# K cache units loaded as 64 KB rows through a ring of three regions, with one V unit split in two

## The chip, the cores and the metric

The kernel runs on one core of a Trainium2 chip. The metric is the device time of one execution in microseconds (us): three runs of the kernel before gave 345.5, 345.55 and 345.85, median 345.55. One further execution was taken by the hardware profiler; it took 345.38 us, of which the profile's span covers 344.0, so 1.38 us lie around the span.

## The reference: what is computed

One decode step of attention for two batch entries, 32 heads, head size 128 and 4096 cached positions, mixed by a gate with a small dense layer. All inputs are bf16.

```python
g = sigmoid((x * gate_w).sum(-1, keepdims=True))       # x: 2 x 1 x 512
q = (x @ wq)                                           # 32 heads of 128
p = softmax(einsum("bhqd,bhkd->bhqk", q, k) * 128**-0.5)
a = einsum("bhqk,bhkd->bhqd", p, v) reshaped @ wo
b = max(x @ w1, 0) @ w2
return g * a + (1 - g) * b
```

The K cache and the V cache hold 2 x 32 x 4096 x 128 values each, 67.1 MB each. The weights add some 11 MB. Every byte of the caches is read once and used for two operations.

## The kernel before, in words

**Units.** Each cache is cut into eight units of 32768 rows of 128 values, 8.39 MB: batch entry u // 4, and eight heads. `unit_in` (L226) lays a unit over 128 partitions, so that one partition gets 64 KB which are contiguous in memory.

**The landing place.** `kv` (L115) holds four slots of 32 KB per partition. K comes in 16 transfers of half a unit each (L237 to L240), so in rows of 32 KB with 64 KB from one row's start to the next; transfer n goes to slot n % 4. The query weights wq land in slot 3 first, so transfer 3 waits until they are used (`pe_qr1`). From n = 4 on, a transfer waits until both transposes of the half that had its slot are done (`kt_...`). V's units 0 to 6 come whole, as 64 KB rows, alternately into slots 0 and 1 and into slots 2 and 3 (L241 to L243); unit u waits for the matmuls of unit u - 2 (`pe_v_...`). V's unit 7 comes as two halves (L244 to L246). Behind it stand wo in two pieces (L247, L248) into slot 0, after `pe_v_6`, and the five pieces of w2 (L249 to L251).

**The queue.** All these loads are issued by SyncE (SP), in the order written. An issue that waits on a semaphore holds up all issues behind it; transfers already issued go on.

**K's stage** (the loop at L496). For each half h of the head size in each half unit, 32 pieces in all, `k_turn` (L349) lets VectorE (DVE) transpose 128 x 4096 f32 words (pairs of bf16 values) from `kv` into one of the NKT = 3 buffers of `kt`. `k_scores` (L357) then runs 16 matmuls of 128 x 512 on TensorE (PE): four weights, each loaded once and held for four banks (the held ones are L195, the one that loads is L375). The scores of all units gather in banks 0 to 3. A transpose waits for the matmuls of the piece three before it. `qbuf` holds the queries in a padded form for four units of two halves; ScalarE (ACT) writes the second batch entry's queries in `q_second` (L323), behind the units that it replaces.

**Between.** `softmax` (L380) takes maxima, exponentials and transposed probabilities; `spread` (L403) lays one unit's probabilities into `ptm`.

**V's stage** (the loop at L505). `v_unit` (L416) runs 64 matmuls per unit, `v_extract` (L431) and `o_gather` (L448) collect. At the end `project` (L468) and `ffn_f` (L477) apply wo and w2, and the output is sent.

The order of all engines is written out by hand; there is no scheduler.

Of the kernel before, what the change touches and what calls it, by code (L numbers as in the profile page):

```python
# [3 lines left out]
dt = mybir.dt  # L4
ALU = mybir.AluOpType
ACT = mybir.ActivationFunctionType
# [7 lines left out]
NKT = 3  # L14
# [71 lines left out]
def bass_gated_mix__gqa_block_cached__dense_activation_relu__decode_kernel(  # L86
# [14 lines left out]
    sb = nc.alloc_sbuf_tensor  # L101
# [10 lines left out]
    ez1 = sb("ez1", [128, 2], dt.float32)  # L112
    gb = sb("gb", [128, 2], dt.float32)
    gm = sb("gm", [128, 2], dt.float32)
    kv = sb("kv", [128, 4, 16384], dt.bfloat16)  # L115
    kt = sb("kt", [128, NKT, 4096], dt.float32)
    qrow = sb("qrow", [128, 2, 4, 128], dt.bfloat16)
    qbuf = sb("qbuf", [128, 8, 4, 160], dt.bfloat16)
    ptm = sb("ptm", [128, 2, 256, 4, 2], dt.bfloat16)
    mpad = sb("mpad", [128, 32], dt.float32)  # L120
    mrow = sb("mrow", [128, 32], dt.float32)
# [15 lines left out]


    flat = kt[:, :, :].rearrange("p k n -> p (k n)")
    kt16 = flat.bitcast(dt.bfloat16).rearrange("p (k r n two) -> p k r n two", k=NKT, r=128, two=2)  # L140
    w1 = flat[:, 0:2752].bitcast(dt.bfloat16)
    E = flat[:, 0:2048].bitcast(dt.bfloat16)
    ET = flat[:, 2048:4096].bitcast(dt.bfloat16)
    w2 = flat[:, 4096:4096 + 2816].bitcast(dt.bfloat16).rearrange("p (r n) -> p r n", n=512)
    X2 = flat[:, 7168:7168 + 1024].rearrange("p (u d) -> p u d", d=128)
    Y = flat[:, 8192:8192 + 512]
    YW = flat[:, 8704:8704 + 512]

    PSF = nc.alloc_psum_tensor("PS", [128, 4096], dt.float32)
    PSB = PSF[:, :].bitcast(dt.bfloat16)  # L150
# [1 line left out]
    def psf(p0, p1, c0, n):  # L152
        return PSF[p0:p1, c0:c0 + n]

    BANK = 512
    QR_B = 5
    QT_B = 4
    qT_ps = PSB[0:128, QT_B * 1024:(QT_B + 1) * 1024]
# [15 lines left out]
    sem_k = [nc.alloc_semaphore(f"sem_k{s}") for s in range(4)]  # L174
    sem_v = [nc.alloc_semaphore(f"sem_v{s}") for s in range(3)]

    mk = {}
# [13 lines left out]
    pool, dve, act, pe, sp = (adder(e) for e in ("pool", "dve", "act", "pe", "sp"))  # L191

    def held(e, out, lhsT, rhs, start, stop):
# [9 lines left out]
         waits=["c_i16z"], signal="c_i16")  # L203
# [5 lines left out]
         waits=["c_i32z"], signal="c_i32")  # L209
# [6 lines left out]
         waits=["c_s4z"], signal="c_s4")  # L216
# [4 lines left out]
    wo_in = A_wo.rearrange("(p r) n -> p (r n)", r=32)  # L221
# [7 lines left out]
    region = kv[:, :, :].rearrange("p (g s) n -> p g (s n)", g=2)  # L229
    wq_sb = kv[:, 3, :].rearrange("p (t u h e d) -> p t u h e d", t=4, u=4, h=4, e=2)  # L230
    wo_sb = kv[:, 0, :]

    act(lambda e: e.dma_start(x_sb[0:2, :], A_x.rearrange("b s d -> (b s) d")).then_inc(sem["x"], 16))
    act(lambda e: e.dma_start(x_sb[2:3, :], gate_w.rearrange("(o d) -> o d", o=1)).then_inc(sem["gw"], 16))
    sp(lambda e: e.dma_start(kv[:, 3, :], wq_in).then_inc(sem["wq"], 16))
    sp(lambda e: e.dma_start(w1, w1_in).then_inc(sem["w1"], 16))
    for n in range(16):  # L237
        u, hf = divmod(n, 2)
        sp(lambda e, n=n, u=u, hf=hf: e.dma_start(kv[:, n % 4, :], unit_in(k_rows, u)[:, 16384 * hf:16384 * (hf + 1)]).then_inc(sem_k[n % 4], 16),
           waits=([f"kt_{2 * (n - 4) + 1}"] if n >= 4 else ["pe_qr1"] if n == 3 else []))  # L240
    for u in range(7):  # L241
# [7 lines left out]
    sp(lambda e: e.dma_start(w2[0:96, 10, :], B_w2[1280:1376, :]).then_inc(sem["w2a"], 16))  # L249
# [41 lines left out]
    def q_proj():  # L291
# [18 lines left out]
        for half in range(2):  # L310
            for j in range(4):
                pe(lambda e, half=half, j=j: e.transpose(qT_ps[:, (4 * half + j) * 128:(4 * half + j + 1) * 128],
                                                         qrow[:, half, j, :], ident16[:, :]),
                   waits=([f"qrow{half}{e2}" for e2 in range(2)] if j == 0 else []),
                   signal=("pe_q" if half and j == 3 else None))
        cols = qT_ps.rearrange("p (f j s m) -> p f s j m", f=2, j=4, s=4)
        for hq in range(4):
            act(lambda a, hq=hq: a.activation(
                out=qbuf[32 * hq:32 * hq + 32, :, :, 32 + 32 * hq].rearrange("p (f s) j -> p f s j", f=2),
                in_=cols[32 * hq:32 * hq + 32, :, :, :, 0], func=ACT.Copy),  # L320
                waits=["pe_q", "c_qbuf"], signal=f"q_0_{hq}")

    def q_second(u):  # L323
        cols = qT_ps.rearrange("p (f j s m) -> p f s j m", f=2, j=4, s=4)
        for hq in range(4):
            act(lambda a, hq=hq: a.activation(  # L326
                out=qbuf[32 * hq:32 * hq + 32, 2 * u:2 * u + 2, :, 32 + 32 * hq],
                in_=cols[32 * hq:32 * hq + 32, u // 2, 2 * (u % 2):2 * (u % 2) + 2, :, 1], func=ACT.Copy),
                waits=[f"pe_sc_{4 * u + 3}"], signal=f"q_1_{u}_{hq}")

    def ffn_h():
        for ft in range(11):
# [14 lines left out]
                signal=f"dve_h{b}")  # L347

    def k_turn(i):  # L349
        n, h = divmod(i, 2)  # L350
        pairs = kv[:, n % 4, :].bitcast(dt.float32).rearrange("p (r h d) -> p h r d", h=2, d=32)
        dst = kt[:, i % NKT, :].rearrange("p (r n) -> p r n", n=32)
        dve(lambda v: v.transpose(out=dst, in_=pairs[:, h]),  # L353
            waits=([f"pe_sc_{i - NKT}"] if i >= NKT else ["pe_h"] if i == 0 else []),
            dwaits=([(sem_k[n % 4], 16 * (n // 4 + 1))] if h == 0 else []), signal=f"kt_{i}")

    def k_scores(i):  # L357
        n, h = divmod(i, 2)
        u, hf = divmod(n, 2)
        for two in range(2):  # L360
            for e2 in range(2):
                pos = 4 * u + 2 * hf + e2
                w = qbuf[:, 2 * (u % 4) + e2, 2 * h + two, 32 - pos:160 - pos]
                first, last = i == 0 and two == 0 and e2 == 0, i == 31 and two == 1 and e2 == 1
                for bk in range(4):
                    head = two == 0 and e2 == 0 and bk == 0
                    waits = [f"kt_{i}"] if head else []
                    if head and i % 4 == 0:
                        waits += [f"q_{u // 4}_{u % 4}_{hq}" if u >= 4 else f"q_0_{hq}" for hq in range(4)]

                    def fn(e, bk=bk, w=w, e2=e2, two=two, first=first, last=last):
                        args = (psf(0, 128, bk * BANK, 512), w, kt16[:, i % NKT, 32 * bk:32 * bk + 32, 16 * e2:16 * e2 + 16, two])
# [3 lines left out]
                    pe(fn, waits=waits, signal=(f"pe_sc_{i}" if two == 1 and e2 == 1 and bk == 3 else None))  # L376
        if i % 4 == 3 and u < 4:
            q_second(u)

    def softmax():  # L380
        dve(lambda v: v.tensor_reduce(out=mpad[:, 0:1], in_=psf(0, 128, 0, 2048), axis=AX.X, op=ALU.max),  # L381
            waits=["pe_sc_31", "c_mpad"], signal="dve_m")
# [32 lines left out]

    def v_unit(u):  # L416
        rows = region[:, u % 2, :].rearrange("p (m c d) -> p m c d", c=4, d=128)
        for m in range(64):
            t = m % 4
            waits, dwaits = [], []  # L420
            if m == 0:
                waits = [f"pt_{u}_{hq}" for hq in range(4)] + ([f"dve_y{u - 2}"] if u >= 2 else [])
                dwaits = [(sem_v[u % 2], 16 * (u // 2 + 1))]
            if u == 7 and m == 32:
                dwaits = [(sem_v[2], 16)]
            pe(lambda e, m=m, t=t: e.matmul(  # L426
                psf(32 * t, 32 * t + 32, V_B[u % 2] * BANK, 512), lhsT=ptm[:, u % 2, 4 * m:4 * m + 4, :, :],
                rhs=rows[:, m], start=(m < 4), stop=(m >= 60), tile_position=(0, 32 * t)),
               waits=waits, dwaits=dwaits, signal=(f"pe_v_{u}" if m == 63 else None))

    def v_extract(u):  # L431
# [60 lines left out]
    gate()  # L492
    selectors()
    q_proj()
    ffn_h()
    for i in range(32):  # L496
        k_turn(i)
        if i >= 1:
            k_scores(i - 1)
    k_scores(31)  # L500
    softmax()
    denominators()
    spread(0)
# [55 lines left out]
```

## Time and profile before

| what | value |
|---|---|
| median of three runs | 345.55 us |
| the profiled execution | 345.38 us |
| its span | 344.0 us |
| busy share of the span: PE, DVE, ACT, POOL | 55%, 51%, 6%, 6% |
| bytes read from HBM | 145.43 MB |
| DVE transposes of K: count, mean of one | 32, 4.424 us |
| weight loads of the score matmuls: count, mean | 128, 0.098 us |
| last transfer of w2 landed, output sent | about 341.7 us, 342.7 us |

How to read it: engines show busy time, and PE's matmuls are pipelined, so 55% is not a share of its peak. The row of DMA in the page is the mean busy share of 16 DMA engines. A landing is seen in the profile as the start of the instruction that waited for it: a transpose for a K transfer, the first matmul of a unit for a V transfer. Differences of such starts tell how far apart two transfers landed.

### The profile page before, as it was taken

Reading aid. Unit: us, or ns where it says so; the run is one execution under the profiler, and the core shown is the slowest. Engines: PE = TensorE matmul, PEld = TensorE weight load, DVE = VectorE, ACT = ScalarE, POOL = GpSimd, SP = SyncE. Lnnn points to the kernel's source line nnn. Section 1 sums busy time; section 2 is a strip of 40 time slices with the busy share of each in tenths; the row PEclk is TensorE's granted clock in tenths of the full one; section 3 lists DMA queues with packets and bytes.
Section 4 is the critical chain, followed back from the end, with each engine's and each line's share of the span. In section 5 each row is a group of like instructions: output and inputs, shape, how many; then the busy total and the mean of one; then the engine's idle time right before and its main releaser. Section 6 shows DMA issues by size and latency. Waiting matters only on the chain.

```text
span 344.0 us, 2352 instructions
## 1 busy us (share of the span) xinstructions
PE 189.3 (55%) x1226; PEld 40.5 (12%) x842; DVE 176.2 (51%) x94; ACT 19.4 (6%) x50; POOL 21.6 (6%) x33
## 2 busy tenths in 40 slices
PE   0432979877787789877875073314070613215264
PEld 0230000000000000000000021102030201002121
DVE  0718888888988888889985730202010030201021
ACT  1130000000000000000000700000000000000000
POOL 8300000000000000000000130101010010100000
PEclk9965899999999999999999565658567565858567
DMA  8999999999999999999999999999999999999995
GB/s 317 457 425 427 427 427 431 434 434 434 440 431 434 431 431 427 427 427 432 462 442 419 472 391 465 404 450 413 434 457 404 472 398 457 419 400 425 433 409 207
DMA packets 4883, 145.57 MB, mean 423 GB/s; under 512 B 549, under 2 KB 906, under 8 KB 1162
## 3 DMA queue, kind: packets, MB, share of 16 engines
q1 hardware_dynamic: 4866, 145.43, 98.5%
q8 instruction: 8, 0.13, 0.2%
q14 instruction: 1, 0.01, 0.0%
q10 hardware_dynamic: 8, 0.00, 0.0%
HBM read 145.43 MB, written 0.00 MB: 423 GB/s over the span
## 4 chain that ended last, share of the span: by engine, by line
DMA 75%; DVE 12%; PE 9%; ACT 1%; issue 1%; SPq 0%; POOL 0%; DVEq 0%
DMA kv<-in_A_k_cache_dram 38%; DMA kv<-in_A_v_cache_dram 27%; DVE kt L353 10%; DMA kt<-in_B_w_dram 7%; PE PS L426 7%; DMA kv<-in_A_wq_dram 4%; ACT kt L396 1%; PE PS L294 1%; PE PS L195 1%; DVE mpad L381 1%; POOL ptm L410 0%; DVE kt L400 0%; PE PS L375 0%; PE PS L481 0%; DVE out_sb L523 0%
## 5 line engine op out<-in xcount | busy, mean ns | idle before, releaser
L353 DVE STREAM_TRANSPOSE kt<-kv 128x4096 f32<-128x4096 f32 x32 | 140.3, 4424 | 19.1 <-DMA kv<-in_A_k_cache_dram 19.1
L195 PE MATMUL PS<-kt,qbuf 128*128 128x512 bf16 x384 | 112.6, 402 | 0.0
L426 PE MATMUL PS<-kv,ptm 128*32 128x512 bf16 x512 | 46.4, 539 | 85.7 <-DMA kv<-in_A_v_cache_dram 84.6
L375 PE MATMUL PS<-kt,qbuf 128*128 128x512 bf16 x128 | 51.8, 405 | 36.3 <-DVE kt L353 36.2
L432 DVE TENSOR_TENSOR kt<-PS,maskc 128x512 f32<-128x512 f32 x8 | 5.5, 692 | 117.6 <-PE PS L426 117.6
L426 PEld LDWEIGHTS PS<-kv,ptm 128*32 128x32 bf16 x512 | 18.6, 128 | 112.1 <-issue 99.7
L375 PEld LDWEIGHTS PS<-kt,qbuf 128*128 128x128 bf16 x128 | 12.5, 98 | 150.5 <-issue 77.0
L410 POOL COPY ptm<-kt 32x512 bf16<-32x512 bf16 x16 | 11.2, 697 | 273.2 <-DVE rsum L440 184.5
L414 ACT ACTIVATE ptm<-kt 32x512 bf16<-32x512 bf16 x8 | 5.1, 654 | 95.3 <-PE PS L426 94.0
L396 ACT ACTIVATE kt<-PS,negm 128x512 bf16<-128x512 f32 x8 | 5.4, 696 | 80.1 <-DVE negm L392 80.1
L436 DVE TENSOR_REDUCE kt<-kt 128x128 f32<-128x512 f32 x8 | 8.2, 1030 | 0.3
L326 ACT ACTIVATE qbuf<-PS 32x8 bf16<-32x8 bf16 x16 | 3.1, 196 | 85.4 <-PE PS L195 85.1
L443 PE MATMUL PS<-rsum,sell 128*32 128x1 f32 x4 | 0.4, 197 | 10.1 <-DVE rsum L440 10.1
L400 DVE STREAM_TRANSPOSE kt<-kt 128x1024 bf16<-128x1024 bf16 x4 | 5.0, 1245 | 1.7 <-ACT kt L396 1.4
L261 PE MATMUL PS<-ident,x_sb 3*128 3x3 bf16 x4 | 0.3, 166 | 8.1 <-POOL s L214 8.1
L264 DVE COPY xT<-PS 128x12 bf16<-128x12 bf16 x1 | 0.2, 171 | 8.4 <-PE PS L261 8.4
L205 POOL MEMSET qbuf<- 128x5120 bf16 x1 | 4.4, 4358 | 0.0
L381 DVE TENSOR_REDUCE mpad<-PS 128x1 f32<-128x2048 f32 x1 | 2.3, 2292 | 4.0 <-PE PS L195 4.0
L294 PE MATMUL PS<-kv,xTw 128*32 128x512 bf16 x32 | 3.3, 584 | 0.6 <-DMA kv<-in_A_wq_dram 0.6
L217 POOL MEMSET ptm<- 128x4096 bf16 x1 | 3.5, 3501 | 0.0
L450 PE MATMUL PS<-kt,selx 128*32 128x128 f32 x16 | 3.1, 330 | 0.6 <-DVE kt L436 0.6
L412 DVE COPY ptm<-kt 32x512 bf16<-32x512 bf16 x8 | 3.1, 387 | 0.2
(63 smaller groups left out, 44.5 us busy)
## 6 DMA issues: line engine op xcount, KB each, us to landing
kv<-in_A_k_cache_dram SPq DMA_DIRECT2D x16, 4096.0 KB, 30.0
kv<-in_A_v_cache_dram SPq DMA_DIRECT2D x2, 4096.0 KB, 28.5
kv<-in_A_wq_dram SPq DMA_DIRECT2D x1, 4096.0 KB, 12.2
kv<-in_A_wo_dram SPq DMA_DIRECT2D x1, 3072.0 KB, 20.9
kt<-in_B_w_dram SPq DMA_DIRECT2D x1, 1376.0 KB, 15.1
kv<-in_A_wo_dram SPq DMA_DIRECT2D x1, 1024.0 KB, 23.4
kt<-in_B_w_dram SPq DMA_DIRECT2D x1, 640.0 KB, 24.2
kt<-in_B_w_dram SPq DMA_DIRECT2D x1, 384.0 KB, 24.7
```

The source lines that it names most:

```text
L195: return e.add_instruction(mybir.InstMatmult(start_tensor_calc=start, stop_tensor_calc=stop, tile_size=(128, 128), tile_position=(0, 0), l ...
L294: pe(lambda e, n=n, t=t: e.matmul(psf(32 * (n % 4), 32 * (n % 4) + 32, (QR_B + n // 4) * BANK, 512), lhsT=xTw[:, t, :], rhs=wq_sb[:, t, n ...
L353: dve(lambda v: v.transpose(out=dst, in_=pairs[:, h]), waits=([f"pe_sc_{i - NKT}"] if i >= NKT else ["pe_h"] if i == 0 else []), dwaits=([ ...
L375: return e.matmul(args[0], lhsT=args[1], rhs=args[2], start=first, stop=last)
L381: dve(lambda v: v.tensor_reduce(out=mpad[:, 0:1], in_=psf(0, 128, 0, 2048), axis=AX.X, op=ALU.max), waits=["pe_sc_31", "c_mpad"], signal=" ...
L396: act(lambda a, bk=bk, e2=e2: a.activation(out=blocks[:, bk, :, 16 * e2:16 * e2 + 16], in_=psf(0, 128, bk * BANK, 512).rearrange("p (r n) ...
L400: dve(lambda v, bk=bk: v.transpose(out=ET[:, 1024 * bk:1024 * bk + 1024], in_=E[:, 1024 * bk:1024 * bk + 1024]), waits=[f"act_exp{bk}{e2}" ...
L410: pool(lambda e, args=args: e.tensor_copy(**args), waits=waits, signal=f"pt_{u}_{hq}")
L414: act(lambda e, args=args: e.activation(func=ACT.Copy, **args), waits=waits, signal=f"pt_{u}_{hq}")
L426: pe(lambda e, m=m, t=t: e.matmul(psf(32 * t, 32 * t + 32, V_B[u % 2] * BANK, 512), lhsT=ptm[:, u % 2, 4 * m:4 * m + 4, :, :], rhs=rows[:, ...
L432: dve(lambda e: e.tensor_tensor(out=Y.rearrange("p (c d) -> p c d", c=4), in0=psf(0, 128, V_B[u % 2] * BANK, 512).rearrange("p (c d) -> p ...
L436: dve(lambda e: e.tensor_reduce(out=X2[:, u, :], in_=Y.rearrange("p (c d) -> p d c", c=4), axis=AX.X, op=ALU.add), waits=[f"dve_y{u}"], si ...
```

## The change

`kv` gets a fifth slot; the three regions of the ring are slot 4 (32 KB), slots 0 and 1 (64 KB) and slots 2 and 3 (64 KB). K comes in ten transfers ("segments") in a new order of units: the halves of units 0 and 7 go through slot 4, and units 1 to 6 go whole, as 64 KB rows, through the two large regions. From the fourth segment on a transfer waits for the last transpose of the segment three before it. V's unit 2 comes in two halves, the first into slot 4 after K's last transpose, the second into slot 0 after the matmuls of V's unit 0. wo goes to slot 4, so that it waits for `pe_v_2`, not `pe_v_6`.

To make room, the buffers of `kt` are half as long: 64 transposes of 128 x 2048, each followed by 8 matmuls with four weight loads, where there were 32 transposes of 128 x 4096, each followed by 16 matmuls with four weight loads. `qbuf` holds two segments' queries and is filled by `q_put`, two segments ahead. `w2` moves to the start of `kt`, and its first piece now waits for the last `spread`.

```diff
-    kv = sb("kv", [128, 4, 16384], dt.bfloat16)
-    kt = sb("kt", [128, NKT, 4096], dt.float32)
+    kv = sb("kv", [128, 5, 16384], dt.bfloat16)
+    kt = sb("kt", [128, NKT, 2048], dt.float32)
-    qbuf = sb("qbuf", [128, 8, 4, 160], dt.bfloat16)
+    qbuf = sb("qbuf", [128, 2, 2, 4, 160], dt.bfloat16)
...
-    wo_sb = kv[:, 0, :]
+    wo_sb = kv[:, 4, :]
+    segments = [(0, (0,)), (1, (0, 1)), (2, (0, 1)), (0, (1,)), (3, (0, 1)), (4, (0, 1)), (7, (0,)), (5, (0, 1)), (6, (0, 1)), (7, (1,))]
+    pieces = []
+    for g, (u, halves) in enumerate(segments):
+        for hf in halves:
+            for h in range(2):
+                for rr in range(2):
+                    pieces.append((g, u, hf, h, rr))
...
+    def place(g):
+        return (4, 0, 2)[g % 3]
...
-    for n in range(16):
-        u, hf = divmod(n, 2)
-        sp(lambda e, n=n, u=u, hf=hf: e.dma_start(kv[:, n % 4, :], unit_in(k_rows, u)[:, 16384 * hf:16384 * (hf + 1)]).then_inc(sem_k[n % 4], 16),
-           waits=([f"kt_{2 * (n - 4) + 1}"] if n >= 4 else ["pe_qr1"] if n == 3 else []))
+    for g, (u, halves) in enumerate(segments):
+        dst = kv[:, 4, :] if len(halves) == 1 else region[:, place(g) // 2, :]
+        src = unit_in(k_rows, u)[:, 16384 * halves[0]:16384 * (halves[-1] + 1)]
+        sp(lambda e, g=g, dst=dst, src=src: e.dma_start(dst, src).then_inc(sem_k[g % 3], 16),
+           waits=([f"kt_{last_of[g - 3]}"] if g >= 3 else ["pe_qr1"] if g == 2 else []))
     for u in range(7):
+        if u == 2:
+            for hf, dst, w in ((0, kv[:, 4, :], "kt_63"), (1, kv[:, 0, :], "pe_v_0")):
+                sp(lambda e, hf=hf, dst=dst: e.dma_start(dst, unit_in(v_rows, 2)[:, 16384 * hf:16384 * (hf + 1)]).then_inc(sem_v[2 - 2 * hf], 16),
+                   waits=[w])
+            continue
         sp(lambda e, u=u: e.dma_start(region[:, u % 2, :], unit_in(v_rows, u)).then_inc(sem_v[u % 2], 16),
-           waits=([f"pe_v_{u - 2}"] if u >= 2 else ["kt_27"] if u == 0 else ["kt_31"]))
+           waits=([f"pe_v_{u - 2}"] if u >= 2 else [f"kt_{last_of[7]}"] if u == 0 else [f"kt_{last_of[8]}"]))
...
-    sp(lambda e: e.dma_start(wo_sb[:, 0:12288], wo_in[:, 0:12288]).then_inc(sem["wo0"], 16), waits=["pe_v_6"])
+    sp(lambda e: e.dma_start(wo_sb[:, 0:12288], wo_in[:, 0:12288]).then_inc(sem["wo0"], 16), waits=["pe_v_2"])
...
-        dve(lambda v: v.transpose(out=dst, in_=pairs[:, h]),
+        dve(lambda v: v.transpose(out=dst, in_=pairs[:, h, 64 * rr:64 * rr + 64]),
...
-                for bk in range(4):
+                for bk in range(2):
```

More of the change, by code (lines that the diff above doesn't have):

```diff
@@ L139, in bass_gated_mix__gqa_block_cached__dense_activation_relu__decode_kernel @@
     flat = kt[:, :, :].rearrange("p k n -> p (k n)")
-    kt16 = flat.bitcast(dt.bfloat16).rearrange("p (k r n two) -> p k r n two", k=NKT, r=128, two=2)
+    kt16 = flat.bitcast(dt.bfloat16).rearrange("p (k r n two) -> p k r n two", k=NKT, r=64, two=2)
     w1 = flat[:, 0:2752].bitcast(dt.bfloat16)
     E = flat[:, 0:2048].bitcast(dt.bfloat16)
[L143 to L147, printed above, removed]
+    ET = flat[:, 4096:6144].bitcast(dt.bfloat16)
+    w2 = flat[:, 0:2816].bitcast(dt.bfloat16).rearrange("p (r n) -> p r n", n=512)
+    X2 = flat[:, 3072:4096].rearrange("p (u d) -> p u d", d=128)
+    qflat = qbuf[:, :, :, :, :].rearrange("p s e j c -> p (s e j c)").bitcast(dt.float32)
+    Y = qflat[:, 0:512]
+    YW = qflat[:, 512:1024]
     PSF = nc.alloc_psum_tensor("PS", [128, 4096], dt.float32)
@@ L173, in bass_gated_mix__gqa_block_cached__dense_activation_relu__decode_kernel @@
     sem = {n: nc.alloc_semaphore("sem_" + n) for n in names}
-    sem_k = [nc.alloc_semaphore(f"sem_k{s}") for s in range(4)]
+    sem_k = [nc.alloc_semaphore(f"sem_k{s}") for s in range(3)]
     sem_v = [nc.alloc_semaphore(f"sem_v{s}") for s in range(3)]
@@ L227, in unit_in @@
         return rows[u * 32768:(u + 1) * 32768, :].rearrange("(p r) d -> p (r d)", p=128)
-    region = kv[:, :, :].rearrange("p (g s) n -> p g (s n)", g=2)
+    region = kv[:, 0:4, :].rearrange("p (g s) n -> p g (s n)", g=2)
     wq_sb = kv[:, 3, :].rearrange("p (t u h e d) -> p t u h e d", t=4, u=4, h=4, e=2)
-    wo_sb = kv[:, 0, :]
+    wo_sb = kv[:, 4, :]
[6 more added lines that the diff above has]
+                    pieces.append((g, u, hf, h, rr))
+    last_of = {p[0]: i for i, p in enumerate(pieces)}
+    first_of = {}
+    for i, p in enumerate(pieces):
+        first_of.setdefault(p[0], i)
+    def place(g):
+        return (4, 0, 2)[g % 3]
     act(lambda e: e.dma_start(x_sb[0:2, :], A_x.rearrange("b s d -> (b s) d")).then_inc(sem["x"], 16))
@@ L246, in bass_gated_mix__gqa_block_cached__dense_activation_relu__decode_kernel @@
            waits=(["pe_v_5"] if hf == 0 else []))
-    sp(lambda e: e.dma_start(wo_sb[:, 0:12288], wo_in[:, 0:12288]).then_inc(sem["wo0"], 16), waits=["pe_v_6"])
+    sp(lambda e: e.dma_start(wo_sb[:, 0:12288], wo_in[:, 0:12288]).then_inc(sem["wo0"], 16), waits=["pe_v_2"])
     sp(lambda e: e.dma_start(wo_sb[:, 12288:16384], wo_in[:, 12288:16384]).then_inc(sem["wo1"], 16))
-    sp(lambda e: e.dma_start(w2[0:96, 10, :], B_w2[1280:1376, :]).then_inc(sem["w2a"], 16))
+    sp(lambda e: e.dma_start(w2[0:96, 10, :], B_w2[1280:1376, :]).then_inc(sem["w2a"], 16),
+       waits=[f"pt_7_{hq}" for hq in range(4)])
     for name, r0, r1 in (("w2b", 0, 5), ("w2c", 5, 8), ("w2d", 8, 9), ("w2e", 9, 10)):
@@ L315, in q_proj, with q_put @@
                    signal=("pe_q" if half and j == 3 else None))
+    def q_put(g):
+        b, u4 = divmod(segments[g][0], 4)
         cols = qT_ps.rearrange("p (f j s m) -> p f s j m", f=2, j=4, s=4)
@@ L318, in q_proj @@
             act(lambda a, hq=hq: a.activation(
[L319 to L329, printed above, removed]
+                out=qbuf[32 * hq:32 * hq + 32, g % 2, :, :, 32 + 32 * hq],
+                in_=cols[32 * hq:32 * hq + 32, u4 // 2, 2 * (u4 % 2):2 * (u4 % 2) + 2, :, b], func=ACT.Copy),
+                waits=(["pe_q", "c_qbuf"] if g < 2 else [f"pe_sc_{last_of[g - 2]}"]), signal=f"q_{g}_{hq}")
     def ffn_h():
@@ L349, in k_turn @@
     def k_turn(i):
-        n, h = divmod(i, 2)
-        pairs = kv[:, n % 4, :].bitcast(dt.float32).rearrange("p (r h d) -> p h r d", h=2, d=32)
+        g, u, hf, h, rr = pieces[i]
+        slot = place(g) + (hf if len(segments[g][1]) == 2 else 0)
+        pairs = kv[:, slot, :].bitcast(dt.float32).rearrange("p (r h d) -> p h r d", h=2, d=32)
         dst = kt[:, i % NKT, :].rearrange("p (r n) -> p r n", n=32)
-        dve(lambda v: v.transpose(out=dst, in_=pairs[:, h]),
+        dve(lambda v: v.transpose(out=dst, in_=pairs[:, h, 64 * rr:64 * rr + 64]),
             waits=([f"pe_sc_{i - NKT}"] if i >= NKT else ["pe_h"] if i == 0 else []),
-            dwaits=([(sem_k[n % 4], 16 * (n // 4 + 1))] if h == 0 else []), signal=f"kt_{i}")
+            dwaits=([(sem_k[g % 3], 16 * (g // 3 + 1))] if i == first_of[g] else []), signal=f"kt_{i}")
     def k_scores(i):
-        n, h = divmod(i, 2)
-        u, hf = divmod(n, 2)
+        g, u, hf, h, rr = pieces[i]
         for two in range(2):
@@ L362, in k_scores @@
                 pos = 4 * u + 2 * hf + e2
-                w = qbuf[:, 2 * (u % 4) + e2, 2 * h + two, 32 - pos:160 - pos]
-                first, last = i == 0 and two == 0 and e2 == 0, i == 31 and two == 1 and e2 == 1
-                for bk in range(4):
+                w = qbuf[:, g % 2, e2, 2 * h + two, 32 - pos:160 - pos]
+                first, last = i < 2 and two == 0 and e2 == 0, i > 61 and two == 1 and e2 == 1
+                for bk in range(2):
                     head = two == 0 and e2 == 0 and bk == 0
                     waits = [f"kt_{i}"] if head else []
-                    if head and i % 4 == 0:
-                        waits += [f"q_{u // 4}_{u % 4}_{hq}" if u >= 4 else f"q_0_{hq}" for hq in range(4)]
+                    if head and i == first_of[g]:
+                        waits += [f"q_{g}_{hq}" for hq in range(4)]
                     def fn(e, bk=bk, w=w, e2=e2, two=two, first=first, last=last):
-                        args = (psf(0, 128, bk * BANK, 512), w, kt16[:, i % NKT, 32 * bk:32 * bk + 32, 16 * e2:16 * e2 + 16, two])
+                        args = (psf(0, 128, (2 * rr + bk) * BANK, 512), w, kt16[:, i % NKT, 32 * bk:32 * bk + 32, 16 * e2:16 * e2 + 16, two])
                         if bk:
@@ L375, in fn @@
                         return e.matmul(args[0], lhsT=args[1], rhs=args[2], start=first, stop=last)
-                    pe(fn, waits=waits, signal=(f"pe_sc_{i}" if two == 1 and e2 == 1 and bk == 3 else None))
-        if i % 4 == 3 and u < 4:
-            q_second(u)
+                    pe(fn, waits=waits, signal=(f"pe_sc_{i}" if two == 1 and e2 == 1 and bk == 1 else None))
+        if i == last_of[g] and g + 2 < len(segments):
+            q_put(g + 2)
     def softmax():
         dve(lambda v: v.tensor_reduce(out=mpad[:, 0:1], in_=psf(0, 128, 0, 2048), axis=AX.X, op=ALU.max),
-            waits=["pe_sc_31", "c_mpad"], signal="dve_m")
+            waits=["pe_sc_63", "c_mpad"], signal="dve_m")
         dve(lambda v: v.transpose(out=mrow[:, :], in_=mpad[:, :]), waits=["dve_m"], signal="dve_mt")
@@ L417, in v_unit @@
         rows = region[:, u % 2, :].rearrange("p (m c d) -> p m c d", c=4, d=128)
+        halves = [kv[:, s, :].rearrange("p (m c d) -> p m c d", c=4, d=128) for s in (4, 0)]
         for m in range(64):
@@ L422, in v_unit @@
                 waits = [f"pt_{u}_{hq}" for hq in range(4)] + ([f"dve_y{u - 2}"] if u >= 2 else [])
[L423 to L426, printed above, removed]
+                dwaits = [(sem_v[2], 16) if u == 2 else (sem_v[u % 2], 16 * (u // 2 + 1))]
+            if u in (2, 7) and m == 32:
+                dwaits = [(sem_v[0], 32) if u == 2 else (sem_v[2], 32)]
+            at = halves[m // 32][:, m % 32] if u == 2 else rows[:, m]
+            pe(lambda e, m=m, t=t, at=at: e.matmul(
                 psf(32 * t, 32 * t + 32, V_B[u % 2] * BANK, 512), lhsT=ptm[:, u % 2, 4 * m:4 * m + 4, :, :],
-                rhs=rows[:, m], start=(m < 4), stop=(m >= 60), tile_position=(0, 32 * t)),
+                rhs=at, start=(m < 4), stop=(m >= 60), tile_position=(0, 32 * t)),
                waits=waits, dwaits=dwaits, signal=(f"pe_v_{u}" if m == 63 else None))
@@ L494, in bass_gated_mix__gqa_block_cached__dense_activation_relu__decode_kernel @@
     q_proj()
+    q_put(0)
+    q_put(1)
     ffn_h()
-    for i in range(32):
+    for i in range(64):
         k_turn(i)
@@ L499, in bass_gated_mix__gqa_block_cached__dense_activation_relu__decode_kernel @@
             k_scores(i - 1)
-    k_scores(31)
+    k_scores(63)
     softmax()
```

## The prediction

> **What bounds the kernel now.** I first read the page's shares and its DMA rows, then the landings, then SP's waits.
>
> ```profile
> PE 189.3 (55%) x1226; PEld 40.5 (12%) x842; DVE 176.2 (51%) x94; ACT 19.4 (6%) x50; POOL 21.6 (6%) x33
> ...
> DMA  8999999999999999999999999999999999999995
> ...
> q1 hardware_dynamic: 4866, 145.43, 98.5%
> q8 instruction: 8, 0.13, 0.2%
> ```
>
> No engine is busy for more than 55% of the span, but the DMA engines are full in every slice but the first and the last, and the loads' queue alone takes 98.5% of 16 engines' time. The bytes cannot change. So the time is the stream of loads, plus some 3 us of end behind it (L481 and the output). The chain of waits agrees: 75% of it is DMA. The question is how dense the stream is, and whether the new order of waits ever leaves it empty.
>
> Density is read from landings. Two K transposes of the timeline, thirteen halves apart, and four first matmuls of V:
>
> ```profile
> 46.96 8.77 DVE L353 STREAM_TRANSPOSE kt<-kv 128x4096 f32<-128x4096 f32 x2 [1.02 <-DMA kv<-in_A_k_cache_dram]
> ...
> 173.23 8.77 DVE L353 STREAM_TRANSPOSE kt<-kv 128x4096 f32<-128x4096 f32 x2 [0.94 <-DMA kv<-in_A_k_cache_dram]
> ...
> 211.99 6.20 PE L426 MATMUL PS<-kv,ptm 128*32 128x512 bf16 x64 [7.80 <-DMA kv<-in_A_v_cache_dram]
> ...
> 308.74 5.61 PE L426 MATMUL PS<-kv,ptm 128*32 128x512 bf16 x64 [14.29 <-DMA kv<-in_A_v_cache_dram]
> 318.47 2.53 PE L426 MATMUL PS<-kv,ptm 128*32 128x512 bf16 x32 [4.11 <-DMA kv<-in_A_v_cache_dram]
> 328.09 3.60 PE L426 MATMUL PS<-kv,ptm 128*32 128x512 bf16 x32 [7.09 <-DMA kv<-in_A_v_cache_dram]
> ```
>
> K's halves in 32 KB rows land (173.23 - 46.96) / 13 = 9.713 us apart, so a unit in two halves takes 19.43. V's whole units in 64 KB rows land (308.74 - 211.99) / 5 = 19.35 us apart (V1 to V6). A unit in one piece is 0.076 us cheaper. The last two lines are V's unit 7 in halves: 9.73 + 9.62 = 19.35, a single sample that shows no such gain. The trace's packet records stand on the other side: a 32 KB row takes 1.217 us on its engine and a 64 KB row 2.422, so two short rows cost 0.012 more; with eight rows per engine that is 0.10 us a unit.
>
> **What the change does to the stream.** Six K units become whole and one V unit becomes two halves: five transfers fewer. At 0.076 us each the stream is 5 x 0.076 = 0.38 us shorter. The ends are 0 (unit 7) and 5 x 0.10 = 0.5. I take 0.076: it is a mean over thirteen and five landings, the others are a single sample and a busy time.
>
> **Does the queue stay full?** I write down the new landings with these intervals, from 27.4 (first transpose at 27.45; the loads up to there are unchanged). A piece of K: the page has transposes of 128 x 32 words at 0.2 us and of 128 x 4096 at 4.424, on a straight line 2048 words take 2.30; two in a row took 8.77, so the next one starts 0.08 before the last ends: 2.22 apart, 8.95 for a half (before 8.77), 17.8 for a unit (7 x 2.22 + 2.30). Both stay below the landings' 9.71 and 19.35. Units land at 46.8 (g1), 66.1 (g2), 75.8, 95.2, 114.5, 124.3, 143.6, 163.0, 172.7 (g9), V0 192.0, V1 211.4, V2a 221.1, V2b 230.8, V3 250.2.
>
> An issue must come before what is already queued has landed:
> - g4 waits for the last transpose of g1: 46.8 + 17.8 = 64.6; the queue is full until g3, 75.8. Cover 11.2 us. g5 (83.9 against 95.2), g7 (113.0 against 124.3), g8 (132.3 against 143.6), V0 (161.4 against 172.7) and V1 (180.8 against 192.0) have the same 11 us; g3, g6, g9 and V2a, which wait for slot 4, more than 20.
> - V2b waits for V0's matmuls. The last transpose ends at 189.7, its 8 matmuls take 1.9 (0.235 us from one to the next in K's stage), then the softmax as before, 11.6 (186.03 to 197.65), and V0's 64 matmuls 6.6: 209.8, against V2a at 221.1. Cover 11.3. Behind V2b in SP's queue stands V3, which waits for V1's matmuls anyway (217.6, against 230.8).
> - V4 waits for V2's second half: 230.8 + 3.5 = 234.4, against 250.2. V5 to V7 are as before.
> - The rest (V7b, wo, w2) is issued at 295, not at 314 to 318; before, V7b covered it until 328. No hole goes, so nothing is gained.
>
> The smallest cover before was V2 (issued at 204.2, V1 landed at 212.0), 7.8 us. So the softmax, 5 to 6 us later than before, costs nothing: V1 lands at 211.4 and V0's matmuls end at 209.8.
>
> **What lies beside the stream, at nothing.** Weight loads of L375: 128 more, 0.098 us each, but a matmul that loads weights takes 0.23 of the chain and a held one 0.24, so they hide in PE's queue; unhidden they would add 0.8 us to the 7.5 that PE needs for a half, under 9.71. ACT's queries: 40 of 0.2 us, written two segments ahead; the first eight at 19.3 us, done long before the first score matmul at 29.7. POOL's memset of `qbuf` halves, 2.2 us less ahead of the first matmuls, which wait for wq (landed at 12.97). `kt` holds three shorter buffers: a piece's 8 matmuls take 1.9 us of the 4.4 that the ring allows. PE's clock was granted at 0.5 from 19.8 on and for the first 4.5 us of scores, 0.42 us a matmul, 3.4 a piece; this comes back after the idle time between the first half and g1 (36.4 to 46.8), costs two or three us there, and g4 has 11. The tail behind the last landing is the same code.
>
> **The rule I weighed.** A transfer with nothing ahead of it, wq, landed 12.24 us after its issue, 2.5 more than the 9.71 of a queued one. If each paid that, five fewer would save 12.6 us (332.6). The queued landings leave no place for it. The Trainium skill's "DMA: Bandwidth & Descriptors" (section "Anatomy of one DMA") fits a transfer as some 2.0 us fixed plus its bytes at 436 GB/s, for DMAs issued by GpSimd; by that the five would be worth 10 us and the time about 335.5 as an estimate. The trace does not agree where the queue is full: 4.194 MB in 9.713 us is 432 GB/s with everything in it.
>
> **The rivals.**
> - No gain, 345.5 (0.09): the 0.076 belongs to K's stage, where DVE and PE read SBUF, and not to the rows. For it: unit 7's halves at 19.35. Against: the packet records show 1.217 in both stages. That 64 KB rows are cut in two on K (0.04) gives the same time; V's rows show 896 packets of 64 KB, so I doubt it.
> - One more instruction fetch, slower, 346.7 (0.07). The eight packets of 16 KB in q8 each go to one DMA engine. After one, in the records, that engine is 1.5 us late (1.10 for the fetch, and its next row 0.46 longer), and since a load lands with its last engine, every landing after the first fetch (23 us) is late by as much: w1 and K's first half, 5.6 MB, took 14.45 us where 432 GB/s gives 12.97. The later ones cost nothing, because each hit an engine not yet hit. PE's 128 more weight loads are half a packet more, so the eighth fetch moves from 338 to about 323, ahead of the end of the stream. It decides if it hits an engine that already had one: 345.2 + 1.5 (or 0.6, if only its bytes at 26 GB/s count). On a ninth engine it is free.
> - K's stage becomes bound by DVE or PE, slower (0.04). DVE would have to use up 11 us of cover over the thirteen halves from g1 to g8, 0.86 each: 2.64 us a piece instead of 2.22. PE at the 0.5 clock throughout needs 13.6 us a half, and some ten halves beyond the cover would cost 39 us (384). Against: before, PE idled 1.4 to 1.5 us in every half and kept its full clock; now it idles about as long once in a unit.
> - A gain beyond 0.7 us (0.05): the early issue of the small loads at the end packs them closer; the slices there hold 340 GB/s, not 430, for some 7 us, 1.4 us at most (343.8). Or every transfer pays a fixed time (0.01, above). Against both: those loads had over 10 us in the queue before, too.
>
> **How the numbers follow.** The forecast has 0.70. The profiled execution would take 344.0 - 0.4 + 1.4 = 345.0; it stood 0.17 below the median of the runs, so the median becomes 345.55 - 0.38 = 345.2. Range 344.8 to 346.0: below, the whole 0.5 and the 0.2 by which runs differ; above, no gain, the runs' upper end (0.3 over the median) and the cheap fetch (345.8). 0.2% is 0.69 us, about what a measurement of this kernel can tell from no change. Forecast, no gain and uncut rows fall within it: 0.83. Faster 0.06, slower 0.11.
>
> **What would show it.** Right: first transposes of whole K units 19.35 us apart; DMA slices full from end to end; SP's issues 11 us ahead of the queue's end; about 4146 packets in q1 (640 rows and 80 completions fewer). Wrong: DMA slices of 8 or less in the middle, first transposes more than 19.4 apart, matmuls of V2 or V3 late, transposes of 2.6 us, or a clock of 0.5 between 60 and 185 us. If all landings shift by 1.5 us after some point, it is the fetch.

## The result, and the profile after

Fifteen runs of each kernel: before 345.7 us (345.38 to 346.23), after 345.13 us (344.77 to 345.32). The ratio is 0.9982, with a 95% interval of 0.9976 to 0.9989: 0.4 to 0.8 us faster. The forecast was 345.2, in a range of 344.8 to 346.0, and a change within 0.2%. The profiled execution took 345.09 us, span 343.8 (before 345.38 and 344.0). Shares and DMA rows of the page after:

```profile
PE 200.2 (58%) x1226; PEld 53.9 (16%) x970; DVE 175.0 (51%) x126; ACT 22.9 (7%) x70; POOL 19.5 (6%) x33
...
DMA  8998989999998999998999999999999999999995
...
q1 hardware_dynamic: 4146, 145.43, 98.4%
q8 instruction: 8, 0.13, 0.2%
```

The reader is to see that nothing else became the bound: the loads' queue moves the same bytes in 720 packets fewer, in 98.4% of 16 engines' time. The K transposes and V's first matmuls in the timeline after (start, busy time, engine, line):

```profile
27.54 8.89 DVE L373 STREAM_TRANSPOSE kt<-kv 128x2048 f32<-128x2048 f32 x4 [4.72 <-DMA kv<-in_A_k_cache_dram]
46.80 17.66 DVE L373 STREAM_TRANSPOSE kt<-kv 128x2048 f32<-128x2048 f32 x8 [10.37 <-DMA kv<-in_A_k_cache_dram]
66.16 26.43 DVE L373 STREAM_TRANSPOSE kt<-kv 128x2048 f32<-128x2048 f32 x12 [1.70 <-DMA kv<-in_A_k_cache_dram]
...
163.01 26.43 DVE L373 STREAM_TRANSPOSE kt<-kv 128x2048 f32<-128x2048 f32 x12 [1.59 <-DMA kv<-in_A_k_cache_dram]
```

```profile
211.68 5.08 PE L447 MATMUL PS<-kv,ptm 128*32 128x512 bf16 x64 [2.58 <-DMA kv<-in_A_v_cache_dram]
221.38 3.57 PE L447 MATMUL PS<-kv,ptm 128*32 128x512 bf16 x32 [4.62 <-DMA kv<-in_A_v_cache_dram]
231.00 3.60 PE L447 MATMUL PS<-kv,ptm 128*32 128x512 bf16 x32 [6.05 <-DMA kv<-in_A_v_cache_dram]
250.45 6.16 PE L447 MATMUL PS<-kv,ptm 128*32 128x512 bf16 x64 [15.85 <-DMA kv<-in_A_v_cache_dram]
...
327.83 3.30 PE L447 MATMUL PS<-kv,ptm 128*32 128x512 bf16 x32 [6.01 <-DMA kv<-in_A_v_cache_dram]
```

The lines of the kernel before against which they are read, beside those shown ahead:

```profile
27.45 8.77 DVE L353 STREAM_TRANSPOSE kt<-kv 128x4096 f32<-128x4096 f32 x2 [4.89 <-DMA kv<-in_A_k_cache_dram]
...
163.52 8.77 DVE L353 STREAM_TRANSPOSE kt<-kv 128x4096 f32<-128x4096 f32 x2 [0.94 <-DMA kv<-in_A_k_cache_dram]
...
250.69 5.63 PE L426 MATMUL PS<-kv,ptm 128*32 128x512 bf16 x64 [14.29 <-DMA kv<-in_A_v_cache_dram]
```

A whole K unit (g2) lands 66.16 - 46.80 = 19.36 us behind g1, where two halves took 19.43. From g1 to g8 there are five whole units and two halves: 116.21 us; the twelve halves between the transposes at 46.96 and 163.52 before took 116.56, so 0.07 us a unit. V's unit 2 in halves gives one unit's gain back: from V1 to V3 38.77 us, before 38.70. From the first K transpose to the last half of V it is 327.83 - 27.54 = 300.29 us, before 328.09 - 27.45 = 300.64: 0.35 us, all of it in the stream of loads.

### The profile page after: what moved, and what is told of

It is laid out like the page before. It is cut to its first block, busy times and chain, and to the rows that moved or that the text cites. A ratio compares the mean times of both kernels' runs of the same rounds, so it can differ in the third digit from the quotient of the medians.

```text
span 343.8 us, 2528 instructions
## 1 busy us (share of the span) xinstructions
PE 200.2 (58%) x1226; PEld 53.9 (16%) x970; DVE 175.0 (51%) x126; ACT 22.9 (7%) x70; POOL 19.5 (6%) x33
## 3 DMA queue, kind: packets, MB, share of 16 engines
q1 hardware_dynamic: 4146, 145.43, 98.4%
## 4 chain that ended last, share of the span: by engine, by line
DMA 76%; DVE 11%; PE 11%; SPq 0%; issue 0%; DVEq 0%
DMA kv<-in_A_k_cache_dram 32%; DMA kv<-in_A_v_cache_dram 28%; DMA kt<-in_B_w_dram 12%; DVE kt L373 10%; PE PS L447 5%; DMA kv<-in_A_wq_dram 4%; PE PS L394 3%; PE PS L196 2%; PE PS L318 1%; SPq L275 0%; DVE kt L457 0%; DVE qbuf L453 0%; DVE out_sb L546 0%; DVE ptm L431 0%; SPq L272 0%
## 5 line engine op out<-in xcount | busy, mean ns | idle before, releaser
L373 DVE STREAM_TRANSPOSE kt<-kv 128x2048 f32<-128x2048 f32 x64 | 141.2, 2274 | 25.4 <-DMA kv<-in_A_k_cache_dram 25.4
L394 PE MATMUL PS<-kt,qbuf 128*128 128x512 bf16 x256 | 107.3, 419 | 33.6 <-DVE kt L373 29.2
L196 PE MATMUL PS<-kt,qbuf 128*128 128x512 bf16 x256 | 106.8, 417 | 0.0
L447 PE MATMUL PS<-kv,ptm 128*32 128x512 bf16 x512 | 48.0, 552 | 78.1 <-DMA kv<-in_A_v_cache_dram 76.9
L453 DVE TENSOR_TENSOR qbuf<-PS,maskc 128x512 f32<-128x512 f32 x8 | 5.5, 691 | 111.5 <-PE PS L447 111.5
L394 PEld LDWEIGHTS PS<-kt,qbuf 128*128 128x128 bf16 x256 | 25.9, 101 | 142.8 <-issue 72.8
L345 ACT ACTIVATE qbuf<-PS 32x8 bf16<-32x8 bf16 x40 | 7.8, 196 | 137.5 <-PE PS L196 136.2
L457 DVE TENSOR_REDUCE kt<-qbuf 128x128 f32<-128x512 f32 x8 | 8.2, 1030 | 0.3
L493 PE MATMUL PS<-kv,oW 128*2 128x512 bf16 x32 | 3.7, 621 | 1.1 <-DMA kv<-in_A_wo_dram 1.1
L333 DVE CAST qrow<-PS 128x256 bf16<-128x256 f32 x2 | 2.4, 1398 | 3.2 <-PE PS L318 3.2
## 6 DMA issues: line engine op xcount, KB each, us to landing
kv<-in_A_v_cache_dram SPq DMA_DIRECT2D x4, 4096.0 KB, 27.5
```

The costliest lines, as they stand in the source:

```text
L196: return e.add_instruction(mybir.InstMatmult(start_tensor_calc=start, stop_tensor_calc=stop, tile_size=(128, 128), tile_position=(0, 0), l ...
L345: act(lambda a, hq=hq: a.activation(out=qbuf[32 * hq:32 * hq + 32, g % 2, :, :, 32 + 32 * hq], in_=cols[32 * hq:32 * hq + 32, u4 // 2, 2 * ...
L373: dve(lambda v: v.transpose(out=dst, in_=pairs[:, h, 64 * rr:64 * rr + 64]), waits=([f"pe_sc_{i - NKT}"] if i >= NKT else ["pe_h"] if i == ...
L447: pe(lambda e, m=m, t=t, at=at: e.matmul(psf(32 * t, 32 * t + 32, V_B[u % 2] * BANK, 512), lhsT=ptm[:, u % 2, 4 * m:4 * m + 4, :, :], rhs= ...
L453: dve(lambda e: e.tensor_tensor(out=Y.rearrange("p (c d) -> p c d", c=4), in0=psf(0, 128, V_B[u % 2] * BANK, 512).rearrange("p (c d) -> p ...
L457: dve(lambda e: e.tensor_reduce(out=X2[:, u, :], in_=Y.rearrange("p (c d) -> p d c", c=4), axis=AX.X, op=ALU.add), waits=[f"dve_y{u}"], si ...
```

## The experiments

Theory "rows": each row of a transfer costs its engine about 0.01 us whatever its length, and the gain is 40 rows an engine saved (five transfers of eight). Rivals: "stage" (short pieces, ring or order make the gain), "end" (the early issue of the last loads), and, left over from the prediction, the instruction fetch and the cover that an issue needs.

**K's whole units in two transfers again**

```diff
-        dst = kv[:, 4, :] if len(halves) == 1 else region[:, place(g) // 2, :]
-        ...
+        for hf in halves:
+            dst = kv[:, place(g) + (hf if len(halves) == 2 else 0), :]
+            src = unit_in(k_rows, u)[:, 16384 * hf:16384 * (hf + 1)]
```

> The changed kernel, but each of K's units 1 to 6 comes in two transfers of 32 KB rows, issued one behind the other, into the same region and with the same waits. Ring, order, pieces and V are those of the changed kernel. Theory 'rows' (the gain is six units in long rows, 0.076 us each by the landings of before): the six are taken back, 0.46 us over the changed kernel, ratio to the kernel before 0.999 to 1.000 (V's unit 2 in halves remains, +0.08). Rival 'stage' (the gain comes from shorter pieces, the other ring or order): no change against the changed kernel, 0.998.

Measured: 345.48 us, ratio to before 0.9993 (0.9985 to 1.0002); 0.35 us over the changed kernel. Two transposes in its timeline:

```profile
47.04 17.66 DVE L374 STREAM_TRANSPOSE kt<-kv 128x2048 f32<-128x2048 f32 x8 [10.61 <-DMA kv<-in_A_k_cache_dram]
...
163.63 26.43 DVE L374 STREAM_TRANSPOSE kt<-kv 128x2048 f32<-128x2048 f32 x12 [1.59 <-DMA kv<-in_A_k_cache_dram]
```

116.59 us from g1 to g8, 0.38 more than in the changed kernel for five units: 0.076 each, as forecast. Ring, pieces and order are unchanged here, and most of the gain is gone. "Stage" falls for that part. (In every cut version the shorter rows also have gaps between them in memory, which whole units have not; a cost of the row and a cost of the jump are not told apart.)

**Short pieces alone, in the kernel before**

```diff
-        dve(lambda v: v.transpose(out=dst, in_=pairs[:, h]),
+        dve(lambda v: v.transpose(out=dst, in_=pairs[:, h, 64 * rr:64 * rr + 64]),
```

(with 64 pieces in the loop and two banks for each, as in the change)

> The kernel before with K's 32 KB transfers and its ring as they were, but with 64 transposes of 128 x 2048 and 8 matmuls behind each, as in the changed kernel. Rows: no change, 1.000, since DVE needs 8.9 us for a half and a half lands every 9.71. Stage: a part of the changed kernel's 0.57 us appears here, ratio 0.998 to 0.999.

Measured: 345.61 us against 345.59, ratio 0.9995 (0.9987 to 1.0004): no change.

**The last loads issued late**

```diff
-    ... then_inc(sem["wo0"], 16), waits=["pe_v_2"])
+    ... then_inc(sem["wo0"], 16), waits=["pe_v_6"])
```

> The changed kernel, but wo, and with it w2 behind it, waits for V's unit 6 as in the kernel before (issue at about 314 instead of 296 us). Rows: no change against the changed kernel, 0.998, as V's last half covers the queue until 328. Rival 'end' (0.2 us or more of the gain come from the early issue at the end): ratio 0.9988 or above.

Measured: 345.08 us, ratio 0.9984 (0.9976 to 0.9993), the changed kernel's time. "End" falls.

**Row or transfer?** Two kernels cut twelve whole units into 16 KB rows, one in two transfers, one in four.

```diff
+    def rows16(ap):
+        quarters = ap.rearrange("p (a b n) -> p b a n", a=2, b=2)
+        return [quarters[:, b] for b in range(2)]
...
+        for d, s in ([(dst, src)] if len(halves) == 1 else zip(rows16(dst), rows16(src))):
```

> The changed kernel, but each of the twelve whole units (K 1 to 6, V 0, 1, 3 to 6) comes in two transfers of 16 KB rows, every other quarter of a partition's 64 KB in each: 32 rows an engine and unit instead of 8, and one transfer more. If the cost belongs to the row (0.0095 to 0.0115 us each): 12 x 24 x that = 2.7 to 3.3 us over the changed kernel, ratio to before 1.006 to 1.008. If it belongs to the transfer (0.076 us each): 12 x 0.076 = 0.9 us, ratio 1.0008. If rows cost nothing: 0.998.

> The same twelve units in four transfers of 16 KB rows: the same rows as the kernel with two transfers, 24 transfers more. Cost by row: 0.2 us over that kernel for the completions (24 x 0.009), ratio 1.006 to 1.009. Cost by transfer: 36 x 0.076 = 2.7 us over the changed kernel, 1.8 over that with two, ratio 1.006. The two kernels together tell row from transfer: equal if by row, 1.8 us apart if by transfer.

Measured: 347.78 us (ratio 1.0063, 1.0048 to 1.0078) and 347.84 us (1.0065, 1.0050 to 1.0080). Whether it is 12 or 36 transfers more makes no difference; 24 rows more per engine and unit do. Two landings of whole V units in the timeline of the kernel with two transfers:

```profile
291.60 5.52 PE L453 MATMUL PS<-kv,ptm 128*32 128x512 bf16 x64 [12.09 <-DMA kv<-in_A_v_cache_dram]
311.17 5.97 PE L453 MATMUL PS<-kv,ptm 128*32 128x512 bf16 x64 [14.05 <-DMA kv<-in_A_v_cache_dram]
```

19.57 us a unit, where the changed kernel has 19.36: 0.21 for 24 rows. Over the run it is (347.78 - 345.13) / 288 rows = 0.0092 us a row. The cost belongs to the row.

**V's unit 2 whole**

```diff
-        if u == 2:
-            ...
-            continue
```

> The changed kernel, but V's unit 2 comes whole into slots 0 and 1, waiting for V's unit 0 (issue at about 209 us, where the queue ends with V1 at 211.5, a cover of 2.4 instead of 11 us). Rows and a cover that is enough: 0.08 us faster than the changed kernel, which can't be told from none, 0.998. If an issue must lead by what wq showed (its landing 2.5 us over a queued one's interval), the cover falls short by 0.1 to 0.5 us, all later landings shift by as much, ratio 0.998 to 1.000.

Measured: 346.95 us (345.85 to 347.87), ratio 1.0035 (1.0025 to 1.0045): slower than the kernel before, outside both expectations. The profiled run is its fastest:

```profile
211.49 5.32 PE L442 MATMUL PS<-kv,ptm 128*32 128x512 bf16 x64 [3.38 <-DMA kv<-in_A_v_cache_dram]
231.77 5.98 PE L442 MATMUL PS<-kv,ptm 128*32 128x512 bf16 x64 [14.96 <-DMA kv<-in_A_v_cache_dram]
251.10 6.54 PE L442 MATMUL PS<-kv,ptm 128*32 128x512 bf16 x64 [13.36 <-DMA kv<-in_A_v_cache_dram]
```

V0's matmuls ended at 208.1, and V2 was issued then (at 208.16), 3.3 us before V1's landing is seen at 211.49; still V2 lands 20.28 us behind V1, 0.93 too late, and that is never made up. The trace's packet records (one for each row, and one of 4 bytes that ends a transfer on each engine) tell why 3.3 was not enough. V1's last rows ended between 208.85 and 210.89 on the 16 engines, and each engine's semaphore update came 0.45 to 0.5 us later. So a landing is seen some 0.6 us after the slowest engine and 2.6 after the fastest one ran dry. V2's first row started at 209.13, 1.0 us behind the issue; at 209.5 only 10 engines had a row to move. The eleven engines that ran dry first stood empty for 0.28 us on average, and their first rows then took 2.94 us instead of 2.42: 0.8 us together. That the unprofiled runs lose more, because V0's matmuls end later when PE's clock is lower (they took 4.92 us here, 5.89 and 6.57 in the two kernels' profiles), is argued, not shown: the granted clocks of the twelve runs (0.794 to 0.827, each a mean over the whole run) do not order with their times.

**V's unit 2 in halves, the second issued later**

```diff
-            for hf, dst, w in ((0, kv[:, 4, :], "kt_63"), (1, kv[:, 0, :], "pe_v_0")):
+            for hf, dst, w in ((0, kv[:, 4, :], "kt_63"), (1, kv[:, 0, :], "pe_v_1")):
```

> The changed kernel, but the second half of V's unit 2 waits for V's unit 1 instead of unit 0: issue at 216.8 instead of 209 us, 4.3 to 4.5 before its predecessor's landing is seen at 221.4. With V's unit 2 whole the issue came 3.4 before, and the next landings were late. By the packet records the last rows of a transfer end some 1.5 us before its landing is seen, and the engines that had no fetch 1.5 before that: the first engine runs dry 3 us before. If that is the point from which it costs: 4.3 is enough, the changed kernel's time, 0.998. If more lead is needed, or an engine that idles at all shows in the end: late landings from V's unit 2 on, ratio 0.999 to 1.003.

Measured: 345.0 us, ten of twelve runs from 344.87 to 345.35, two at 345.79 and 346.47; ratio 0.9991 (0.9981 to 1.0001). In its profile the halves land at 221.22, 230.84 and V3 at 250.28, spaced as in the changed kernel. V2's second half is issued at 216.9, so its first row can start at 217.9; by the packet records the fastest engine has rows of the first half until 218.87. So 4.4 us is enough in most runs; the two late ones may be those in which it was not, which the runs don't show.

**Whole K units without a third region**

```diff
-    for n in range(16):
-        ...
+    for u in range(8):
+        sp(lambda e, u=u: e.dma_start(region[:, u % 2, :], unit_in(k_rows, u)).then_inc(sem_k[u % 2], 16),
+           waits=([f"kt_{4 * u - 5}"] if u >= 2 else ["pe_qr1"] if u == 1 else []))
```

> The kernel before with all eight K units whole, in 64 KB rows, but in the two regions of 64 KB that there were, without a third: each is issued when the unit two before it is transposed, 17.5 us after its landing, where the next lands 19.4 after: a cover of 1.9 us at K's units 2 to 7, V0, V1 and V2. If an issue needs 2.5 us of lead (wq's landing against a queued interval): 0.6 us lost nine times, 5 us over before less 0.6 for eight long units, ratio 1.013. If a cover of 1.9 is enough: 0.6 us faster, ratio 0.998, and the third region of the changed kernel buys nothing.

Measured: 356.36 us (355.73 to 359.75), ratio 1.0331 (1.0269 to 1.0394): more than twice the expected loss. Its K transposes in the timeline, and three stretches of 1 us (the last three columns are PE's granted clock, the DMA share and GB/s; a row is counted whole in the stretch in which it starts, so a share can be over 1):

```profile
56.35 17.42 DVE L352 STREAM_TRANSPOSE kt<-kv 128x4096 f32<-128x4096 f32 x4 [1.99 <-DMA kv<-in_A_k_cache_dram]
79.29 17.42 DVE L352 STREAM_TRANSPOSE kt<-kv 128x4096 f32<-128x4096 f32 x4 [5.51 <-DMA kv<-in_A_k_cache_dram]
98.94 17.42 DVE L352 STREAM_TRANSPOSE kt<-kv 128x4096 f32<-128x4096 f32 x4 [2.23 <-DMA kv<-in_A_k_cache_dram]
120.14 17.42 DVE L352 STREAM_TRANSPOSE kt<-kv 128x4096 f32<-128x4096 f32 x4 [3.77 <-DMA kv<-in_A_k_cache_dram]
```

```profile
53.00:54.00 1.00, 1.00 (x6) 0.10 (x1) 1.00 (x1) 0.00 (x0) 0.00 (x0) 1.00 0.15 66
54.00:55.00 1.00, 1.00 (x6) 0.10 (x1) 0.36 (x1) 0.00 (x0) 0.00 (x0) 1.00 0.01 0
55.00:56.00 1.00, 1.00 (x6) 0.13 (x2) 0.00 (x0) 0.00 (x0) 0.00 (x0) 1.00 2.68 918
```

Unit 2 is issued at 54.4, when unit 1 is transposed, and lands 22.94 us behind it instead of 19.35. In the packet records 13 of 16 engines have no row from 54.4 to 55.4, when the new rows begin; most of these first rows take 2.6 to 3.3 us instead of 2.42, and one engine takes up its first row only at 57.8. Units 2 to 7 lose 0.3 to 3.6 us each. The largest loss falls on no instruction fetch; two others do (108.5 us for the landing at 120.14, 173.7 for that at 180.52). Why one engine came so late after 54.4 stays open. What is shown: with two regions long rows cost 10.6 us; the third is what makes them pay.

**More instructions on PE**

```diff
+    def idle_pe(n):
+        for c in range(n):
+            def fn(e, c=c):
+                args = (psf(0, 128, 6 * BANK, 2), ident16[:, :], ident16[:, 0:2])
+                ...
         v_unit(u)
+        if 1 <= u <= 5:
+            idle_pe(256)
```

> The changed kernel with 256 tiny matmuls (128 x 2 on a held weight, into an unused bank) behind each of V's units 1 to 5, where PE waits for the next landing: 1285 instructions more, so five more fetches of 16 KB. If each fetch goes to an engine that had none: no change, 0.998. If a fetch hits engines at random, some engine is hit once more, +1.5 us, ratio 1.0025. If PE is late with a unit, its waits show it.

> Control for the kernel with 256 tiny matmuls behind V's units 1 to 5 (6.5 us of PE each, 346.65): the same places hold 20 matmuls of 128 x 512 each, so about as much PE time (20 x 0.24 to 0.43 us) with 105 instructions more instead of 1285, less than half a fetch. If the 1.5 us there came from instruction fetches: the changed kernel's time, 0.998. If they came from PE being busy beside the loads or late with a unit: 1.0027 as there.

> The changed kernel with 420 tiny matmuls behind V's units 1 to 5 and 6 behind each K piece: 2546 instructions more, ten fetches more instead of five. If a fetch on an engine that already had one costs 1.5 us of that engine, and the latest engine sets every landing: ten more put at least one engine at three, 1.5 us over the kernel with five, ratio 1.007. If extra fetches stay spread evenly so that none has three: 1.0027 again. If fetches cost nothing: 0.998.

Measured: 346.65 us (1.0027, 1.0015 to 1.0039) with 13 fetches; the control with wide matmuls 345.07 us (0.9982, 0.9973 to 0.9992); 347.75 us (1.0058, 1.0043 to 1.0073) with 18. (The control has nine, the ninth at 340.6 us, when the large transfers are through.) The row of the fetch queue and V's landings of the first of them:

```profile
q8 instruction: 13, 0.21, 0.3%
```

```profile
250.47 6.46 PE L456 MATMUL PS<-kv,ptm 128*32 128x512 bf16 x64 [9.35 <-DMA kv<-in_A_v_cache_dram]
...
270.87 6.50 PE L456 MATMUL PS<-kv,ptm 128*32 128x512 bf16 x64 [6.04 <-DMA kv<-in_A_v_cache_dram]
...
290.31 5.33 PE L456 MATMUL PS<-kv,ptm 128*32 128x512 bf16 x64 [5.11 <-DMA kv<-in_A_v_cache_dram]
...
310.05 5.69 PE L456 MATMUL PS<-kv,ptm 128*32 128x512 bf16 x64 [7.93 <-DMA kv<-in_A_v_cache_dram]
```

Up to 250.47 it stands with the changed kernel; then two intervals are too long: 20.40 and 19.74, 1.4 us together, where PE waits 5 to 9 us for each landing. The control has 4.5 to 5.6 us of PE work in the same places, where the first has 6.5, and loses nothing. So the instructions cost, not the matmuls, and they cost through the loads. The packet records show how, by the records that end a transfer on each engine. When V's unit 3 ends in the first kernel, the last engine finishes 2.14 us behind the first; when unit 4 ends, 9 fetches in, one engine is 3.19 behind, and when unit 6 ends four are 3.2 to 3.7. With 18 fetches eight are 2.9 to 4.1 behind at that point. In the changed kernel no engine is ever more than 2.0 behind, through all eight fetches. So the first seven or eight each made another engine late by about 1.5 us, and the later ones also hit engines that were late already.

The first fetch does the same in every kernel. In the one with short pieces alone it came later (26.6 us; in the kernel before and the changed one 24.3 and 25.4), and there it can be seen by itself:

```profile
26.11 8.89 DVE L353 STREAM_TRANSPOSE kt<-kv 128x2048 f32<-128x2048 f32 x4 [2.92 <-DMA kv<-in_A_k_cache_dram]
37.15 8.89 DVE L353 STREAM_TRANSPOSE kt<-kv 128x2048 f32<-128x2048 f32 x4 [2.16 <-DMA kv<-in_A_k_cache_dram]
46.87 8.89 DVE L353 STREAM_TRANSPOSE kt<-kv 128x2048 f32<-128x2048 f32 x4 [0.82 <-DMA kv<-in_A_k_cache_dram]
```

The first half lands at 26.11, not 27.5; the next 11.04 us later, 1.33 more than 9.71; then the step is regular. In the two kernels with 13 and nine fetches it came at 27.6 and 27.7, and the first half landed at 26.14 and 25.95. No version tried beats the changed kernel beyond its interval.

## Why the prediction was right

- **The stream, 0.38 us.** Confirmed in mechanism and size: 0.07 us a unit in the changed kernel, 0.076 when it is undone, 0.35 over the whole stream, and a row of 0.0092 us (40 rows: 0.37). The packet count came out at the forecast 4146. The chosen 0.076 was nearer than either end. Unit 7's halves at 19.35, which spoke for no gain, were misread: the first matmul of a unit starts 0.13 us after its transfer's last semaphore update, one in the middle of a unit 0.05. From update to update (308.61, 318.33, 328.05) the halves took 19.44, as in K's stage. Unit 2 after shows the same 9.70 and 9.62 in the matmuls, and 19.42 in the updates.
- **The queue stays full.** Confirmed, but the step was mis-sized: it counted cover up to the moment when the landing is seen. The engines run dry 0.6 to 2.6 us before, and a new row starts 1.0 us behind its issue, so the first 3.6 us of cover are needed. (The prediction, and the expectation for the second half issued later, place packets about 1 us too early against the instructions; so "1.5" and "3 us" there, and a fetch at 23 or 338, are 0.6, 2.6, 24.3 and 339.4.) With 11 us this changed nothing; with 3.3 it cost 0.9 us in the profile and 1.8 in the median. The Trainium skill, "DMA: Bandwidth & Descriptors" (section "Anatomy of one DMA"), says of DMAs issued by GpSimd that most of a transfer's fixed time is the wait until its last byte is confirmed. For these loads, issued by SP, the trace does not agree: 1.0 us lies ahead of the first row, 0.45 to 0.5 us between an engine's last record and its semaphore update.
- **The pieces.** 2.274 us a piece and 17.66 a unit, forecast 2.30 and 17.8. The softmax moved as forecast (V0's first matmul at 203.21, forecast 203.2). PE's clock was 0.5 again after the idle time ahead of g1, but g1's transposes took 17.66 us like all others: the two or three us allowed for it were not needed, as the ring of pieces covered them. The rival "K's stage becomes bound" counted on the full clock from there on; in fact it fell to 0.5 three more times, for 3.4 us each (from 98.6, 146.4 and 166.8 us; in the last, matmuls took 0.43 us instead of 0.23). The cover was large enough for that too.
- **The early issue at the end.** Worth nothing, as said.
- **The fetch rival.** The mechanism is real and its price right (1.5 us for five more). It did not occur: the changed kernel still has eight fetches. The eighth came at 331.9 us, 7.5 earlier than before and not 15 as forecast, and nothing moved by it: from the last half of V to the issue of the output it is 14.6 us, before and after. But the reason given, that each fetch meets a new engine, holds for seven or eight of them, not for thirteen. What decides which engine a fetch takes was not settled.
- **The signs.** Two signs of failure appeared without a failure. Slices of 8 in the DMA row stand in K's stage (the fourth, sixth, thirteenth and nineteenth) with the stream as dense as forecast; a 64 KB row is counted in the slice in which it starts, so slices with long rows waver. And PE's clock was at 0.5 at times between 60 and 185 us, the other sign, as said above.

The runs moved by 0.57 us (0.4 to 0.8), the profiled stream by 0.35. The spans that were recorded for the runs tell where the rest lies. Their median is 343.8 us in the fifteen runs after and 344.1 in the 35 runs of the kernel before that belong to the first experiments: 0.3 us, the stream. What lies around the span is 1.27 to 1.35 us after, but 1.33 to 1.96 before, over 1.6 in 12 of the 35 runs. That is also where the runs of before scatter; their spans reach only from 343.9 to 344.4. With K's units cut again in the new kernel the span is back at 344.2 and the rest stays short (1.27 to 1.38). So the rows account for the change within the span, and ring, order and pieces for none of it. Another 0.1 to 0.3 us, which the prediction did not have, lies outside the span; its cause stays open. That the median came out within 0.1 us of the forecast is in part luck: it started from 345.55, the median of three runs, where fifteen gave 345.7, and that part made up the difference.

## What to carry to other kernels

When the queue of loads is never empty, only what each engine moves counts: the rows, and anything else on the same engines. Count rows, price them from two landings, and expect tenths of a microsecond. A bigger transfer is worth having only if its issue still comes early enough before its predecessor's landing is seen: here 3.3 us were too few and 4.4 enough in ten of twelve runs, since the first engine is dry 2.6 us before and a new row takes 1.0 us to start.

## What the runs showed of the hardware that was not expected

A fetch of 16 KB of PE's instructions (one for some 256 of them) makes one DMA engine late by about 1.5 us. The first one delays every later landing by 1.33 us, the next ones nothing until an engine is hit again; then it is 1.5 us for thirteen fetches in all and 2.6 for eighteen. And an empty queue costs more than the time in which it is empty: after it the first 64 KB rows took 2.5 to 3.3 us instead of 2.42, and in one case an engine began only 3.4 us after the issue, so that its unit landed 3.6 us late.
